# Folding one batch's first FFT stage onto 64x64 tiles, half of it inside a wait, with its input on two DMA queues

## The chip, the cores and the metric

One core of a Trainium2 chip (trn2) runs the whole program. The metric is device time in microseconds (us) of one execution; a time quoted for a kernel is the median of its fast runs, those within 1.5% of its fastest. In the profiles PE is TensorE (PEld its weight loads), DVE is VectorE, ACT ScalarE, POOL GpSimd and SP SyncE; SPq and ACTq are the queues (also rings) on which SP and ACT issue DMAs. Ratios are computed as the mean time of one kernel's fast runs over the mean of the other's fast runs of the same rounds, so they are not quite the ratio of the medians. The numbers in brackets behind a ratio are its 95% interval. Runs of different sessions are compared only through the kernel before, which ran beside each; its median was 904.68 us beside the kernel after, 901.19 beside e1 to e4, 901.86 beside e5 to e7 and 902.24 beside e8 to e11, and its single runs took 903.56 beside e12 and e13 and 908.88 beside e14 and e15.

## The reference, cut to what matters

```python
x: (8, 3008, 256)                      # batch, sequence, channels
X = np.fft.rfft(x, axis=1)             # filters: 1505 x 256
y = np.fft.irfft(X * (filt_r + 1j * filt_i), n=3008, axis=1)
h = y.reshape(24064, 256)
out = (np.maximum(h @ w_gate, 0) * (h @ w_val)) @ w_out    # d_ff 1536
```

The kernel splits 3008 = 94 x 32. Stage A is a 94-point transform (fp32 matmuls on the rows of `x`, one row per partition). Its result goes out to DRAM (`Abuf`) and comes back with the axes exchanged (`at`): this is the **bounce**. Then come a 32-point transform (`psX`), the product with the filters (`tt`, `uu`), the inverse of it (`psD`), a second trip through DRAM (`Dbuf` out, `dC` back), the last inverse step (`psY`), and the FFN (`psV`, `psG`, `psO`). The FFN loop of one batch has the FFT work of the next woven in. Only batch 0 has nothing to hide its FFT behind, and batch 1's A has to be done somewhere near it.

## The kernel before: the parts concerned

```python
def load_x(b, eng, cols):                 # 32 rows on every fourth of all partitions, 8 or 16 KB runs
    for c, c0, c1 in cols:
        for m in range(3):
            rows = min(32, B * N1 - (b * N1 + 32 * m))
            eng.dma_start(XF[c][m:m + 4 * rows - 3:4, c0:c1], ...)

def load_at(b, c):                        # bounce: 384 KB in 512 B pieces
    nc.sync.dma_start(ats[b][c:c + 125:4], _ap(Abuf[b], ..., [[D, 32], [4 * NC2 * D, NG], [1, D]]))
...
load_at(0, 0) ... load_at(0, 3)           # batch 0's four loads of A, on SP's queue
load_x(1, nc.sync, ((0, 0, 2 * q), (0, 2 * q, 4 * q), (1, 0, 4 * q)))     # then batch 1's x, same queue
early = items_a(1)                        # batch 1's A: 32 fp32 matmuls of 512 columns, unfolded
first_b(amid)                             # batch 0: psX, products, psD, with six matmuls of `early` amid
load_d(0, 0, 2)
nc.gpsimd.dma_start(last, ...)            # one row of D: Pool waits for D here
load_vg(DFF // 2, DFF)                    # second half of the gate and value weights
for f in early: f()                       # the remaining 26 matmuls, while D is away
item_c(0, 0); item_c(0, 1)                # psY, then the FFN loop
```

## Time and profile before

| | kernel before |
|---|---|
| median, runs | 903.77 us (900.53 to 905.6, 3 runs before the prediction); 904.68 with a fourth run of 907.75, used for the ratio |
| PE busy in the profiled run | 883.1 of 904.2 us |
| batch 0: end of A / first `psX` | 27.9 / 37.47 us |
| first `psV` (start of the FFN) | 63.38 us |
| first `psX` of batch 1 | 83.22 us |

The first 63 us are a chain of loads, bounce, products and the trip of D. The lines for this stand in the prediction. Two that it does not show: SP's timeline, which has start, length of the issue, operation and tile,

```profile
33.93 0.58 SPq L350 DMA_DIRECT2D at<-Abuf  x1
57.22 1.87 SPq L427 DMA_DIRECT2D dC<-Dbuf  x4
```

The fourth load of A is issued at 33.93, and PE's first `psX` follows at 37.47: it lands in some 3.5 us. SP issues the loads of D at 57.22, when D's last write has landed.

### The profile page before, as it was taken

How to read it: one execution, taken by the hardware profiler on the slowest of the kernel's cores; microseconds unless marked ns; L12 is line 12 of the kernel's file. 1: busy time of each engine (PE TensorE's matmuls, PEld its weight loads, DVE VectorE, ACT ScalarE, POOL GpSimd, SP SyncE). 2: the span in 40 equal slices, each digit the busy share in tenths (PEclk: the TensorE clock that was granted, in tenths of full speed). 3: DMA queues.
4: the chain of work that ended last, by engine and by line, in shares of the span. 5: the costliest groups of instructions: out<-in, count | busy, mean ns of one | idle time of the engine just before them, and what ended most of it. 6: DMA issues, size and time to landing. Idle time of an engine off the chain costs nothing.

```text
span 904.2 us, 19169 instructions
## 1 busy us (share of the span) xinstructions
PE 883.1 (98%) x7198; PEld 510.3 (56%) x7198; DVE 569.6 (63%) x873; ACT 498.8 (55%) x891; POOL 362.2 (40%) x359
## 2 busy tenths in 40 slices
PE   6899999999999999999999999999999999999997
PEld 2334555556555665566655566555655565666665
DVE  2636766467665776657766667666766577655553
ACT  3475555455655565555555565555565555555553
POOL 4242398217680386614864166811768000000001
PEclk9999999999999999999999999999999999999999
DMA  8998358523475344653364533754346512331111
GB/s 227 262 249 174 104 144 178 120 79 101 123 179 115 89 118 125 149 133 106 106 151 130 126 103 92 186 117 102 103 131 168 115 33 79 79 77 36 37 31 52
DMA packets 113554, 109.17 MB, mean 121 GB/s; under 512 B 20327, under 2 KB 98055, under 8 KB 112822
## 3 DMA queue, kind: packets, MB, share of 16 engines
q1 hardware_dynamic: 90294, 80.10, 34.4%
q0 software_dynamic: 22448, 26.41, 11.9%
q8 instruction: 56, 0.92, 0.4%
q10 hardware_dynamic: 720, 1.45, 0.4%
q14 instruction: 36, 0.29, 0.1%
HBM read 61.93 MB, written 49.81 MB: 124 GB/s over the span
## 4 chain that ended last, share of the span: by engine, by line
PE 85%; POOL 5%; DMA 5%; issue 3%; ACT 1%; SPq 1%; DVE 0%; ACTq 0%; POOLq 0%
PE psV L467 25%; PE psO L486 25%; PE psG L467 25%; PE psF L323 3%; PE psY L451 2%; PE psD L394 2%; PE psX L364 1%; DMA XP<-in_x_dram 1%; DMA WgT<-in_moe_w_gate_dram 1%; DMA Dbuf<-dsb 1%; PE psA L276 1%; POOL XP L296 1%; DMA XF<-in_x_dram 1%; POOL fold L309 1%; POOL XP L310 1%
## 5 line engine op out<-in xcount | busy, mean ns | idle before, releaser
L472 DVE SCALAR_TENSOR_TENSOR prod<-psG,vsb 128x512 bf16<-128x512 f32 x564 | 389.4, 690 | 267.5 <-ACT vsb L470 255.0
L470 ACT CAST vsb<-psV 128x512 bf16<-128x512 f32 x564 | 331.9, 588 | 269.4 <-PE psV L467 187.1
L467 PE MATMUL psV<-yT,WvT 128*128 128x512 bf16 x1128 | 337.1, 380 | 1.2 <-ACT yT L456 1.2
L467 PE MATMUL psG<-yT,WgT 128*128 128x512 bf16 x1128 | 336.1, 379 | 1.5 <-DMA WgT<-in_moe_w_gate_dram 0.7
L486 PE MATMUL psO<-WoT,prod 128*128 128x256 bf16 x2256 | 337.0, 273 | 0.0
L486 PEld LDWEIGHTS <-prod 128*128 128x128 bf16 x2256 | 220.8, 98 | 144.1 <-issue 0.8
L467 PEld LDWEIGHTS <-WgT 128*128 128x128 bf16 x1128 | 110.1, 98 | 137.1 <-issue 3.1
L467 PEld LDWEIGHTS <-WvT 128*128 128x128 bf16 x1128 | 98.5, 98 | 42.4 <-issue 30.9
L258 POOL CAST scr<-yT 128x8 f32<-128x8 bf16 x25 | 4.7, 189 | 268.1 <-ACT yT L456 268.1
L509 POOL DMA_DIRECT2D out_dram<-osb x5 | 2.6, 536 | 196.0 <-ACT osb L499 196.0
L380 DVE TENSOR_TENSOR tt<-psX,Ftr 128x512 bf16<-128x512 f32 x96 | 65.1, 683 | 6.7 <-PE psX L364 6.7
L499 ACT COPY osb<-psO 128x512 f32<-128x512 f32 x92 | 53.9, 585 | 27.7 <-PE psO L486 26.8
L309 POOL TENSOR_TENSOR fold<-XP 128x1024 f32<-128x1024 f32 x24 | 56.5, 2356 | 24.2 <-PE psF L323 20.8
L380 DVE TENSOR_TENSOR uu<-psX,Fti 128x512 bf16<-128x512 f32 x89 | 60.6, 681 | 0.0
L401 ACT CAST dsb<-psD 128x512 bf16<-128x512 f32 x96 | 51.5, 589 | 12.5 <-PE psD L394 11.8
L310 POOL TENSOR_TENSOR XP<-XP 128x1024 f32<-128x1024 f32 x24 | 56.4, 2348 | 1.9
L296 POOL DMA_DIRECT2D XP<-in_x_dram x96 | 56.7, 595 | 0.9 <-issue 0.4
L330 DVE CAST asb<-psF 128x512 bf16<-128x512 f32 x48 | 30.9, 686 | 21.3 <-PE psF L323 16.2
L330 ACT CAST asb<-psF 128x512 bf16<-128x512 f32 x48 | 25.8, 589 | 31.2 <-PE psF L323 31.2
L456 ACT CAST yT<-psY 128x512 bf16<-128x512 f32 x47 | 27.5, 585 | 25.3 <-PE psY L451 24.8
L458 DVE CAST yT<-psY 128x512 bf16<-128x512 f32 x47 | 32.0, 681 | 10.8 <-PE psY L451 10.8
L451 PE MATMUL psY<-M,dC 96*128 96x94 bf16 (+18 forms) x604 | 37.5, 198 | 0.1
(69 smaller groups left out, 505.5 us busy)
## 6 DMA issues: line engine op xcount, KB each, us to landing
at<-Abuf SPq DMA_DIRECT2D x32, 384.0 KB
dC<-Dbuf SPq DMA_DIRECT2D x64, 192.0 KB
XP<-in_x_dram POOLq DMA_DIRECT2D x48, 256.0 KB, 5.8
Dbuf<-dsb SPq DMA_DIRECT2D x23, 512.0 KB
XP<-in_x_dram POOLq DMA_DIRECT2D x96, 96.0 KB, 2.7
Abuf<-asb SPq DMA_DIRECT2D x96, 96.0 KB
out_dram<-osb SPq DMA_DIRECT2D x69, 94.0 KB
XF<-in_x_dram SPq DMA_DIRECT2D x15, 256.0 KB
```

Source lines behind the costliest of these rows:

```text
L296: nc.gpsimd.dma_start(xp[r:r + 24, 0:4:2, :], _ap(x, (b * N1 * N2 + o) * D, [[N2 * D, 24], [47 * N2 * D, 2], [1, 512]]))
L309: tt(t, xp[:, 0:2], xp[:, 2:4], op=ALU.add)
L310: tt(xp[:, 2:4], xp[:, 0:2], xp[:, 2:4], op=ALU.subtract)
L330: copy(asf[:, :, q, :], banks[q])
L380: nc.vector.tensor_tensor(p, psX, filt, op=ALU.mult)
L401: nc.scalar.copy(dsb[:, a, o:o + 2, :], psD[a])
L451: nc.tensor.matmul(psY[:, o:o + w], dCs[b, n2 // 8][:, n2 % 8, h * 128:(h + 1) * 128], M1[:, n1:n1 + w], start=True, stop=True)
L467: nc.tensor.matmul(pt[:, :W], w[:, h, ft * 128:(ft + 1) * 128], yt[:, h, :], start=(h == 0), stop=(h == 1))
L470: nc.scalar.copy(vsb, psV[:, :W])
L472: nc.vector.scalar_tensor_tensor(prod, in0=psG[:, :W], scalar=0.0, in1=vsb, op0=ALU.max, op1=ALU.mult)
L486: nc.tensor.matmul(psO[:, t % 2], prods[ft][:, t * 128:(t + 1) * 128], WoT[:, ft, :], start=(ft == 0), stop=(ft == NFT - 1))
L499: copy(osb[:, t0 % 2:t % 2 + 1], psO[:, t0 % 2:t % 2 + 1])
```

## The change

Batch 1's A is to use the symmetry of the real transform (fold rows n and −n into a sum and a difference, which halves the contraction) in four chunks on 64x64 tiles. Two chunks go into the wait for D, two into the FFN. VectorE folds chunks 0 and 1, GpSimd (POOL) folds 2 and 3. Its x is laid out for that: 48 rows for one half of the 32 columns on partitions 0 to 47, the same rows for the other half on partitions 64 to 111. It is split over SP's and ACT's queues, and starts right behind batch 0's third load of A; the fourth load of A moves to ACT's queue. In front, small zeroing and loads for the filters move behind batch 0's x. Filler, or junk, matmuls (`warm`, `psJ`) do no useful work; their results are thrown away.

```diff
+    def load_halves(c, engs):
+        for k in range(2):
+            for h in range(2):
+                engs[h].dma_start(X1[c][64 * h:64 * h + 48, k], _ap(x, ..., [[N2 * D, 48], [8 * D, 2], [1, 4 * D]]))
+    def fold_half(j, eng):
+        eng.tensor_tensor(t, xp[:, 0], xp[:, 1], op=ALU.add)
+        eng.tensor_tensor(xp[:, 1], xp[:, 0], xp[:, 1], op=ALU.subtract)
+    def halves_a(j):                      # sixteen matmuls, tile_position=(64 * h, 64 * e)
...
-    for (src, dst) in FILT:               # moved behind load_x(0, ...)
-        nc.vector.memset(dst[64:128, NG - 2:, :], 0.0)
-    load_own_filters()
...
-    load_x(1, nc.sync, ((0, 0, 2 * q), (0, 2 * q, 4 * q), (1, 0, 4 * q)))
+    load_at(0, 3, nc.scalar)
+    for c in range(2):
+        load_halves(c, (nc.sync, nc.scalar))
...
-    first_b(amid)
+    first_b()                             # filler matmuls in place of the six of A
     load_d(0, 0, 2)
+    for j in range(2):
+        fold_half(j, nc.vector)
+    for j in range(2, 4):
+        fold_half(j, nc.gpsimd)
     (the load named last, load_vg; load_o is now here too)
-    for i, f in enumerate(early): f() ...
+    warm(6)
+    for j in range(2):
+        halves_a(j)
+        warm(4)
...                                       # in the FFN of batch 0
+    for j, e in ((2, 1), (3, 3)):
+        at_step(e, lambda j=j: halves_a(j))
+    at_step(3, lambda: load_at_tiled(1))
```

More of the change, by code (lines that the diff above doesn't have):

```diff
@@ L105, in _tables @@
     fold = np.zeros((128, 4, 32))
+    half1 = np.zeros((128, 4, 32))
     i = np.arange(24)
@@ L115, in _tables @@
             fold[32 * q:32 * q + 24, 2 * odd + 1, 0:24] = np.where(k1 % 47 == 0, 0.0, -np.sin(th))
+        th = 2 * np.pi * (np.outer(np.arange(47) - 23, k1) % N1) / N1
+        for h in range(2):
+            half1[64 * h:64 * h + 47, 2 * odd, 0:24] = np.cos(th)
+            half1[64 * h:64 * h + 47, 2 * odd + 1, 0:24] = np.where(k1 % 47 == 0, 0.0, -np.sin(th))
     tab = np.concatenate([perm, swap, own.reshape(128, -1), m1], 1)
-    return wa.astype(np.float32), fold.reshape(128, 128).astype(np.float32), f2.astype(NBF16), tab.astype(NBF16)
+    fold = np.stack([fold, half1], 1).reshape(128, 256)
+    return wa.astype(np.float32), fold.astype(np.float32), f2.astype(NBF16), tab.astype(NBF16)
 @with_exitstack
@@ L155 @@
     Dbuf = [dram.tile([NROW * N2, D], BF16, name=f"Dbuf{b}") for b in range(B)]
-    XF = [pro.tile([128, NX2 * D], FP32, name=f"XF{c}") for c in range(N2 // NX2)]
+    XF = [consts.tile([128, NX2 * D], FP32, name=f"XF{c}") for c in range(N2 // NX2)]
+    XD = [t[:, :].rearrange("p (k n) -> p k n", k=4) for t in XF]
+    XP = [XD[j // 2][:, :, 512 * (j % 2):512 * (j % 2) + 512] for j in range(4)]
     WA = pro.tile([128, NROW], FP32)
-    WF = consts.tile([128, 4, 32], FP32)
+    WFS = consts.tile([128, 2, 4, 32], FP32)
+    WF, W1 = WFS[:, 0], WFS[:, 1].rearrange("p c k -> p (c k)")
     M1 = consts.tile([NROW, N1], BF16)
@@ L182 @@
     FILT = ((filt_r, Ftr), (filt_i, Fti))
+    junk = pro.tile([128, 512], BF16, tag="junk", bufs=1)
     tabs = pro.tile([128, tab_h.shape[1]], BF16, tag="tabs", bufs=1)
@@ L261, with fft_tag @@
     turn = {"tags": ("fft", "psv", "psg", "pso"), "i": 0}
-    def fft_tag(side=False):
-        if side and turn.get("side"):
-            return turn["side"]
+    def fft_tag():
         turn["i"] += 1
@@ L273, in one @@
                 st["asb"] = sb.tile([128, NC2 * D], BF16, tag="asb", bufs=4, name="asb")
-            psA = ps.tile([128, 512], FP32, tag=fft_tag(True), name="psA")
+            psA = ps.tile([128, 512], FP32, tag=fft_tag(), name="psA")
             o = (c * NC2 % NX2) * D + j * 512
@@ L280, in one @@
             if j == 3:
-                eng = nc.scalar if b and c > 1 else nc.sync
-                eng.dma_start(_ap(Abuf[b], c * NROW * NC2 * D, [[NC2 * D, NROW], [1, NC2 * D]]),
+                nc.sync.dma_start(_ap(Abuf[b], c * NROW * NC2 * D, [[NC2 * D, NROW], [1, NC2 * D]]),
                                   st["asb"][:NROW])
@@ L306, in fold_chunk @@
         xp = XP[j]
-        t = fs.tile([128, 2, 512], FP32, tag="fold", bufs=2, name="fold")
+        t = sb.tile([128, 2, 512], FP32, tag="fold", bufs=2, name="fold")
         tt = nc.gpsimd.tensor_tensor
@@ L325, in tiled_a, with store_a @@
                                  tile_position=(r, 32 * c))
+        store_a(b, j, banks, (nc.scalar.copy, nc.vector.tensor_copy) * 2)
+    def store_a(b, j, banks, copies):
         asf = sb.tile([128, NC2 * D], BF16, tag="asb", bufs=4, name="asb")
@@ L328, in tiled_a @@
         for q in range(4):
-            copy = nc.scalar.copy if q % 2 == 0 else nc.vector.tensor_copy
-            copy(asf[:, :, q, :], banks[q])
+            copies[q](asf[:, :, q, :], banks[q])
         for c in range(4):
@@ L342, in load_at_tiled, with load_at @@
                                   [[D, 32], [N2 * D, 24], [1, D]]))
-    POOL_U = ((0, 1), (1, 0), (1, 1), (2, 0), (2, 1), (3, 1), (4, 0))
+    X1 = [t[:, :].rearrange("p (k q n) -> p k q n", k=2, q=2) for t in XF]
+    def load_halves(c, engs):
+        for k in range(2):
+            for h in range(2):
+                engs[h].dma_start(X1[c][64 * h:64 * h + 48, k],
+                                  _ap(x, ((N1 + 47 * k) * N2 + 16 * h + 4 * c) * D,
+                                      [[N2 * D, 48], [8 * D, 2], [1, 4 * D]]))
+    def fold_half(j, eng):
+        xp = X1[j // 2][:, :, :, 2 * D * (j % 2):2 * D * (j % 2) + 2 * D]
+        pool, tag = (pro, "half") if j < 2 else (sb, "fold")
+        t = pool.tile([128, 2, 2 * D], FP32, tag=tag, bufs=2, name="half")
+        eng.tensor_tensor(t, xp[:, 0], xp[:, 1], op=ALU.add)
+        eng.tensor_tensor(xp[:, 1], xp[:, 0], xp[:, 1], op=ALU.subtract)
+        fold[1, j] = (t, xp[:, 1])
+    def halves_a(j):
+        banks = [ps.tile([128, 2, D], FP32, tag=t, name="psF") for t in ("psv", "psg", "fft", "fft")]
+        for q in range(2):
+            for h in range(2):
+                for e in range(2):
+                    nc.tensor.matmul(banks[2 * h + q][64 * e:64 * e + 64],
+                                     W1[64 * h:64 * h + 48, 64 * e:64 * e + 64],
+                                     fold[1, j][e][64 * h:64 * h + 48, q], start=True, stop=True,
+                                     tile_position=(64 * h, 64 * e))
+        store_a(1, j, banks, (nc.scalar.copy,) * 4 if j < 2 else (nc.scalar.copy, nc.vector.tensor_copy) * 2)
+    POOL_U = ((0, 1), (1, 0), (1, 1), (2, 1), (3, 0), (3, 1))
     ats = {}
-    def load_at(b, c):
+    def load_at(b, c, eng):
         if c == 0:
             ats[b] = sb.tile([128, NG, D], BF16, tag="at", bufs=1, name="at")
-        nc.sync.dma_start(ats[b][c:c + 125:4],
+        eng.dma_start(ats[b][c:c + 125:4],
                           _ap(Abuf[b], c * NROW * NC2 * D, [[D, 32], [4 * NC2 * D, NG], [1, D]]))
@@ L354, with fwd @@
     CUTS = (0, 2, 4, 6)
-    def fwd(b, i):
+    def fwd(b, i, junks=False):
         for e in range(2):
-            psXs[b, i, e] = ps.tile([128, 2, D], FP32, tag=fft_tag(), name="psX")
+            tag = "fft" if b or not e else "psv"
+            psXs[b, i, e] = ps.tile([128, 2, D], FP32, tag=tag, name="psX")
+            for _ in range(2 * junks):
+                nc.tensor.matmul(psXs[b, i, e], junk[:, 0:128], junk, start=True, stop=True)
         for m in range(2):
@@ L381, in product, with inv @@
         tus[b, i, e, k] = p
-    def inv(b, i, tags=None, cuts=CUTS):
+    def inv(b, i, tags, cuts=CUTS):
         if i in cuts:
@@ L387, in inv @@
         i0, dsb = dsbs[b]
-        psD = [ps.tile([128, 2, D], FP32, tag=tags[a] if tags else fft_tag(), name="psD")
+        psD = [ps.tile([128, 2, D], FP32, tag=tags[a], name="psD")
                for a in range(2)]
@@ L404, in inv, with first_b @@
                               dsb[:, :, :o + 2, :])
-    def first_b(amid):
-        cuts = (0, 2, 4, 5, 6)
+    def first_b():
+        cuts, tags = (0, 2, 4, 5, 6), ("psg", "pso")
         for i in range(6):
-            fwd(0, i)
+            fwd(0, i, True)
             if i > 1:
-                inv(0, i - 2, cuts=cuts)
+                inv(0, i - 2, tags, cuts)
             for e in range(2):
@@ L415, in first_b @@
                 product(0, i, e, 1, pool=(i, e) in POOL_U)
-            amid(i)
-        inv(0, 4, cuts=cuts)
-        amid(6)
-        inv(0, 5, cuts=cuts)
+        for i in range(4, 6):
+            inv(0, i, tags, cuts)
     dCs = {}
@@ L511, in o_part @@
                                           osb[o + c0:o + c1, tt % 2])
-    junk = pro.tile([128, 512], BF16, tag="junk", bufs=1)
     def warm(n, cols=512):
-        psJ = ps.tile([128, 512], FP32, tag=fft_tag(True), name="psJ")
+        psJ = ps.tile([128, 512], FP32, tag=fft_tag(), name="psJ")
         for i in range(n):
@@ L538 @@
     load_x(0, nc.sync, ((0, 0, q), (0, q, 2 * q), (0, 2 * q, 4 * q), (1, 0, 2 * q), (1, 2 * q, 4 * q)))
-    nc.sync.dma_start(WF, nc.inline_tensor(fold_h, name="dft_fold").ap())
+    nc.sync.dma_start(WFS, nc.inline_tensor(fold_h, name="dft_fold").ap())
+    for (src, dst) in FILT:
+        nc.vector.memset(dst[64:128, NG - 2:, :], 0.0)
+    load_own_filters()
     hold_gpsimd(XF[0][:, 2 * q - 8:2 * q])
@@ L547 @@
         if i == 12:
-            load_at(0, 0)
-            load_at(0, 1)
-    for c in range(2, 4):
-        load_at(0, c)
+            load_at(0, 0, nc.sync)
+            load_at(0, 1, nc.sync)
+    load_at(0, 2, nc.sync)
     for half in range(2):
@@ L564 @@
     place_nyq()
-    for i in range(11):
+    for i in range(13):
         warm(2)
-    load_x(1, nc.sync, ((0, 0, 2 * q), (0, 2 * q, 4 * q), (1, 0, 4 * q)))
-    early = items_a(1)
-    def amid(i):
-        if i < 2:
-            warm(4, 256)
-        else:
-            for _ in range((1, 1, 2, 1, 1)[i - 2]):
-                next(early)()
+    load_at(0, 3, nc.scalar)
+    for c in range(2):
+        load_halves(c, (nc.sync, nc.scalar))
     hold_gpsimd(ats[0][0:32, NG - 1, 0:8])
     load_vg(0, DFF // 2)
-    turn["tags"], turn["side"] = ("fft", "psv", "psg"), "pso"
-    first_b(amid)
-    turn["tags"], turn["side"] = ("fft", "psv", "psg", "pso"), None
+    first_b()
     load_d(0, 0, 2)
+    for j in range(2):
+        fold_half(j, nc.vector)
+    for j in range(2, 4):
+        fold_half(j, nc.gpsimd)
     nc.gpsimd.dma_start(pro.tile([1, D], BF16, tag="last", bufs=1, name="last"),
@@ L586 @@
     load_vg(DFF // 2, DFF)
-    load_at(1, 0)
-    for i, f in enumerate(early):
-        f()
-        if i == 5:
-            load_at(1, 1)
+    load_o()
+    warm(6)
+    for j in range(2):
+        halves_a(j)
+        warm(4)
     for h in range(2):
         item_c(0, h)
-    hold_gpsimd(yTs[0][:, 0, 0:8])
-    load_o()
     prologue.close()
     fs = ctx.enter_context(tc.tile_pool(name="fs", bufs=2))
-    XP = []
-    def clear_chunks():
-        for i in range(4):
-            XP.append(fs.tile([128, 4, 512], FP32, tag=f"XP{i}", bufs=1, name=f"XP{i}"))
-            nc.gpsimd.memset(XP[i], 0.0)
     turn["tags"] = ("fft",)
@@ L613 @@
     C_AT = (8, 10)
-    at_step(2, clear_chunks)
     for b in range(1, B):
@@ L617 @@
         if b == 1:
-            for c in range(2, 4):
-                at_step(c - 2, lambda c=c: load_at(1, c))
+            for j, e in ((2, 1), (3, 3)):
+                at_step(e, lambda j=j: halves_a(j))
+            at_step(3, lambda: load_at_tiled(1))
         else:
```

## The prediction

> **What bounds the kernel now.** I read the page first. Its busy row and its chain say that TensorE is the bound of the whole run: PE is busy 98% of 904.2 us, and 85% of the chain that ended last is PE work.
>
> ```profile
> PE 883.1 (98%) x7198; PEld 510.3 (56%) x7198; DVE 569.6 (63%) x873; ACT 498.8 (55%) x891; POOL 362.2 (40%) x359
> PE 85%; POOL 5%; DMA 5%; issue 3%; ACT 1%; SPq 1%; DVE 0%; ACTq 0%; POOLq 0%
> ```
>
> So a change can move the end in two ways only: by moving the instant at which the FFN loop starts, or by adding to or taking from PE's time inside the loop. The change touches only the first 100 us or so. I read PE's timeline there, then the waits of PE from 36 to 92 us:
>
> ```profile
> 19.11 8.78 PE L276 MATMUL psA<-XF,WA 128*96 128x512 f32 x16 [2.06 <-DMA XF<-in_x_dram]
> 37.47 0.41 PE L364 MATMUL psX<-at,F 64*64 64x256 bf16 x8 [2.01 <-issue]
> 52.91 8.82 PE L276 MATMUL psA<-XF,WA 128*96 128x512 f32 x20
> 63.38 0.59 PE L467 MATMUL psV<-yT,WvT 128*128 128x512 bf16 x2 [1.18 <-ACT yT L456]
> 83.22 0.41 PE L364 MATMUL psX<-at,F 64*64 64x256 bf16 x8 [0.86 <-issue]
> ...
> PE psG L467 <- DMA WgT<-in_moe_w_gate_dram: 0.7, 1, 0.7
> ```
>
> The FFN starts at 63.38. Before it PE runs batch 1's A (the second psA row): 8.8 us of fp32 matmuls that stand exactly where D of batch 0 goes to memory and back. The chain of waits shows that round trip:
>
> ```profile
> 46.00 7.34 DMA Dbuf<-dsb
> ...
> 54.53 2.67 DMA Dbuf<-dsb
> ...
> 59.06 10.74 DMA WgT<-in_moe_w_gate_dram
> ```
>
> The last write of D lands at 57.2, SP issues the loads of it by 59.1, so D is back near 60 us by my estimate; A ends at 61.7. The two finish almost together: PE's A is hardly longer than the wait it fills. Removing A alone therefore buys at most some 2 us.
>
> [...] eight 64x256 bf16 matmuls (psX) take 0.41 us. [...] No two-SBUF-input op of DVE is in the trace before; its PSUM product of 512 elements takes 0.69, so I estimate 1.15 us for 1024. [...] from 44 to 45 us q1 and q0 moved 28 packets each, but 0.29 and 0.04 MB, so large packets take the bandwidth.
>
> **The change, part by part.**
>
> Front. The zeroing for the filters and their small loads move behind the x loads, so DVE clears the first quarter of XF 0.8 us sooner and POOL, which idled until 1.43 and cleared the second quarter at 4.07 to 5.07, does so about 2.5 us sooner. SP's fourth load waited for that until 5.10; now it can follow the third at about 3.6. From 10 us on the DMA is full (0.99 to 1.19), which limits the gain: some 1.4 us on batch 0's A.
>
> Bounce of batch 0. Batch 1's x no longer queues behind the whole bounce. SP's half follows the third load of A, into a hole: the DMA share from 33 to 35 us is 0.06. But the fourth load of A, issued at 33.93 on SP, goes to ACT's ring, in 512 B packets against x's 4 KB on SP's. By packet-wise turns it gets an eighth while x lasts: I estimate 0.5 to 1.8 us more. With 1.4 gained in front, the first psX starts at 37.3, near the 37.47 of before. The filler added ahead (four plus four junk matmuls) ends by then.
>
> Forward and inverse FFT of batch 0. Six psA (6 x 0.86 = 5.2 us of PE) and their ACT copies (6 x 0.57 = 3.4 us) go, 24 junk matmuls (24 x 0.216 = 5.2 us) come, so PE is even and ACT, busy 13.7 of 18 us, is freed. Pool products fall from 7 to 6. Walking the six rounds by 0.61 us per DVE product, 0.55 per ACT copy and 1.15 per Pool product, the last product ends 13.2 us after the first psX (before: 14.4) and the last inverse 13.9 after. The 7.34 us wait for the first write of D shrinks as x is no longer ahead of it in SP's ring. The last copy of D ends at 51.9 instead of 54.5, its write lands at 54.6, D is back near 57.5.
>
> The wait for D. DVE folds chunks 0 and 1 after its products: 4 x 1.15 = 4.6, from 50.5 to 55.1. POOL folds 2 and 3: 4 x 2.35 = 9.4, from 47 to 56.6. A chunk's matmuls are eight 64x512 fp32 on four tiles, two rounds of 0.86 plus some 0.2 (before, sixteen on 32x32 tiles, one round, took 1.16): 1.9 us. PE: inverse to 51.3, six junk (1.3), chunk 0 to 54.6, four junk (0.9), chunk 1 55.1 to 57, four junk to 57.9, then psY and a copy: FFN at 59.6. The one-row load named last now waits for POOL's folds: issued at 57.2, landing 3.4 later (as before), at 60.6, and the first copy out of psV waits for it. Effective start 60.2: 3.2 us gained.
>
> Inside the FFN. Chunks 2 and 3 add 2 x 1.9 = 3.8 us of PE. Two waits should go: 0.86 for A of batch 1 (written by about 73, wanted near 82) and perhaps the 0.7 for the second half of the gate weights, whose load is issued at the same time as before; the four memsets of POOL (7.1 us) vanish, off the path. The chunk stores are sixteen small DMAs on an SP queue with time to spare.
>
> Sum: -3.2 + 3.8 - 0.9 - 0.5 = -0.8; from there on the loop is the same, instruction for instruction but for line numbers, with the folds of batch 2 on strided views of the same sizes. Total about 903.
>
> **Rivals.** (A) [...] POOL's folds begin at 47 and DVE's at 50.5; if each excludes the other for a whole op, they alternate and DVE's four end near 61 instead of 55. Chunk 1 then ends at 63, the FFN starts at 65, and the total is 907 to 910, more if PE's idle stretch drops the clock. [...] Against: the amounts of filler fit folds of 1.15 us too well, as if chosen from a trace that did not have it. I give it 45%. (B) The granted clock. From 19 to 24 us it was 0.66 after a DMA wait, and again from 166 to 171; at half rate for some 3.5 us each cost about 1.8 us. Other arrival times of x could spare the first or add one: plus or minus 1.8 us. (C) The bounce is slowed more than I think, and all that follows slips: plus 1 to 2. (D) The gate weights come later, because POOL must fold before it can issue them: plus 1 to 3 on the sixth step.
>
> **Range and chances.** Without (A) 901 to 903.5, with it 906 to 910; the clock adds 1.8 either way, and three runs of before spread over 5 us. Median 903; eight in ten between 898 and 909. Two per cent is 18 us; nothing above reaches that, since all that changes lies within the first 85 us, where PE already idles only about 9 us.
>
> **What would show each step.** First psX at 37.3, within 1 (front and bounce); last product 13.2 after it; DVE folds of 1.15 each and back to back (no lock) or with gaps of 2.4 (lock); first psV between 59 and 61 (no lock), 64 to 66 (lock); psF rows of about 1.9 us a chunk; no idle before the psX of batch 1 near 82. I am wrong if DVE's folds stretch in themselves, if psX starts after 39, if the weights stall step 6 for over 1 us, or if the loop after 100 us runs at another pace.

## The result, and the profile after

The kernel after took 918.14 us (917.25 to 918.98, 4 runs) and the kernel before, in the same rounds, 904.68 (900.53 to 907.75, 4 runs). The ratio is 1.0152, with a 95% interval of 1.0108 to 1.0195. Results are correct. The whole interval lies above 1: the change costs 1 to 2%, and the time is 15 us more than predicted.

| us from the start (profiled runs) | before | after | later by |
|---|---|---|---|
| end of batch 0's A | 27.9 | 25.2 | −2.7 |
| first `psX` | 37.47 | 46.51 | +9.0 |
| first `psV` | 63.38 | 77.78 | +14.4 |
| first `psX` of batch 1 | 83.22 | 100.12 | +16.9 |
| end | 904.2 | 915.8 | +11.6 |

PE's timeline of the kernel after, the lines that answer to those in the prediction (start, busy time, line, operation, and in brackets the idle time before it with what ended it):

```profile
18.16 7.08 PE L284 MATMUL psA<-XF,WA 128*96 128x512 f32 x16 [2.47 <-DMA XF<-in_x_dram]
46.51 0.64 PE L408 MATMUL psX<-at,F 64*64 64x256 bf16 x8 [11.15 <-DMA at<-Abuf]
77.78 0.38 PE L509 MATMUL psV<-yT,WvT 128*128 128x512 bf16 x1 [0.25 <-ACT yT L498]
100.12 0.41 PE L408 MATMUL psX<-at,F 64*64 64x256 bf16 x8
```

PE now stands still for 11.15 us ahead of the first `psX`, for a load of A. The chain of waits of the kernel after names which one (start, length, what):

```profile
25.88 6.47 DMA Abuf<-asb
32.35 0.02 issue
32.38 14.09 DMA at<-Abuf
46.47 0.04 issue
46.51 0.70 PE psX L408 x7
```

The load issued at 32.38 is the fourth, on ACT's queue. It takes 14.09 us; before, its twin took some 3.5. What the DMA engines did meanwhile shows in two rows of the windows view of each kernel (window, its length, busy time of PE, PEld, DVE, ACT and POOL, then PEclk, the clock granted to TensorE as a share of full speed, then the mean busy share of the 16 DMA engines, and what all queues together moved in GB/s). First the kernel before:

```profile
36.00:39.00 3.00, 1.53 (x23) 0.91 (x24) 1.09 (x2) 0.00 (x0) 1.20 (x3) 1.00 0.99 324
45.00:48.00 3.00, 2.92 (x28) 1.14 (x29) 2.15 (x4) 2.86 (x6) 2.29 (x3) 1.00 1.02 353
```

Then the kernel after:

```profile
36.00:39.00 3.00, 0.00 (x0) 0.00 (x0) 0.00 (x0) 0.00 (x0) 0.00 (x0) 1.00 1.03 135
45.00:48.00 3.00, 1.49 (x11) 0.56 (x12) 0.81 (x2) 0.00 (x0) 1.11 (x3) 0.50 1.02 212
```

The engines are as full as before (1.03 against 0.99) and move 135 GB/s instead of 324. The DMA view of the kernel after says whose bytes they are (queue, packets, MB, share), first from 34 to 37 us:

```profile
q1 hardware_dynamic: 128, 0.44, 101.7%
q10 hardware_dynamic: 4, 0.00, 0.6%
```

Then from 37 to 40 us:

```profile
q10 hardware_dynamic: 442, 0.23, 64.2%
q1 hardware_dynamic: 67, 0.20, 44.5%
```

q1 is SP's queue with x, q10 is ACT's with the load of A (and ACT's half of x behind it). In the first three us q10 moves 4 packets against 128; in one-us views all four of them fall between 36 and 37, after SP had issued the last of its four loads of x (28.71 to 35.93). In the next three us q10 moves 442 against 67. So the load of A first stood still and then got most of the packets. By an estimate from packets and MB, all but some twenty of its 768 packets had moved by 42 us, but the load is complete only at 46.47. The last row of the windows view above shows the second cost, PEclk at 0.50: TensorE, idle since 35 us, was granted half rate from 42 us on (0.68 from 39 to 42), and was still at 0.62 from 48 to 51.

Later the folds show a third cost. VectorE's timeline:

```profile
59.95 1.22 DVE L369 TENSOR_TENSOR half<-XF 128x1024 f32<-128x1024 f32 x1
61.20 3.25 DVE L370 TENSOR_TENSOR XF<-XF 128x1024 f32<-128x1024 f32 x1
64.37 3.38 DVE L369 TENSOR_TENSOR half<-XF 128x1024 f32<-128x1024 f32 x1
67.78 3.25 DVE L370 TENSOR_TENSOR XF<-XF 128x1024 f32<-128x1024 f32 x1
```

GpSimd's timeline:

```profile
57.67 2.35 POOL L369 TENSOR_TENSOR half<-XF 128x1024 f32<-128x1024 f32 x1
60.10 3.27 POOL L370 TENSOR_TENSOR XF<-XF 128x1024 f32<-128x1024 f32 x1
63.33 3.34 POOL L369 TENSOR_TENSOR half<-XF 128x1024 f32<-128x1024 f32 x1
66.75 3.20 POOL L370 TENSOR_TENSOR XF<-XF 128x1024 f32<-128x1024 f32 x1
```

Only VectorE's first fold, which starts in the tail of POOL's first, has the length that it has alone, 1.22 us. Each later one lasts until the POOL fold beside it ends and then some 1.1 us more: VectorE's four end at 71.03 instead of some 64.8 (59.95 plus four times 1.2). That is rival (A) of the prediction, called the lock from here on: side by side VectorE's folds take 3.25 to 3.38 us (1.22 alone) and POOL's 3.20 to 3.34 (2.35 alone). It shows as longer instructions and not as gaps of 2.4 us between them, which the prediction had told its reader to look for.

### The profile page after: what moved, and what is told of

Same layout as the page of the kernel before. It is cut to its first block, busy times and chain, and to the rows that moved or that the text cites.

```text
span 915.8 us, 19321 instructions
## 1 busy us (share of the span) xinstructions
PE 888.0 (97%) x7264; PEld 510.3 (56%) x7264; DVE 583.3 (64%) x882; ACT 496.2 (54%) x886; POOL 365.7 (40%) x357
## 4 chain that ended last, share of the span: by engine, by line
PE 87%; DMA 4%; POOL 4%; DVE 2%; SPq 1%; issue 1%; ACT 0%; DVEq 0%; POOLq 0%
PE psV L509 26%; PE psG L509 25%; PE psO L528 25%; PE psF L330 3%; PE psY L493 2%; DMA XF<-in_x_dram 2%; PE psD L438 2%; PE psX L408 2%; DMA at<-Abuf 2%; PE psF L379 1%; PE psA L284 1%; SPq L185 1%; DVE XF L370 1%; DMA Abuf<-asb 1%; POOL XF L303 1%
## 5 line engine op out<-in xcount | busy, mean ns | idle before, releaser
L316 POOL TENSOR_TENSOR fold<-XF 128x1024 f32<-128x1024 f32 x24 | 56.5, 2355 | 21.0 <-PE psF L330 20.8
L303 POOL DMA_DIRECT2D XF<-in_x_dram x96 | 56.6, 595 | 1.6 <-PE psG L509 1.2
L317 POOL TENSOR_TENSOR XF<-XF 128x1024 f32<-128x1024 f32 x24 | 56.4, 2348 | 1.9
L340 ACT CAST asb<-psF 128x512 bf16<-128x512 f32 x60 | 32.2, 589 | 40.8 <-PE psF L330 28.7
L340 DVE CAST asb<-psF 128x512 bf16<-128x512 f32 x52 | 33.5, 686 | 20.8 <-PE psF L330 11.6
L498 ACT CAST yT<-psY 128x512 bf16<-128x512 f32 x47 | 27.5, 585 | 25.2 <-PE psY L493 25.0
L493 PEld LDWEIGHTS <-dC 96*128 96x128 bf16 x604 | 34.9, 98 | 3.5 <-issue 1.1
```

What stands on the lines that cost most here:

```text
L303: nc.gpsimd.dma_start(xp[r:r + 24, 0:4:2, :], _ap(x, (b * N1 * N2 + o) * D, [[N2 * D, 24], [47 * N2 * D, 2], [1, 512]]))
L316: tt(t, xp[:, 0:2], xp[:, 2:4], op=ALU.add)
L317: tt(xp[:, 2:4], xp[:, 0:2], xp[:, 2:4], op=ALU.subtract)
L340: copies[q](asf[:, :, q, :], banks[q])
L493: nc.tensor.matmul(psY[:, o:o + w], dCs[b, n2 // 8][:, n2 % 8, h * 128:(h + 1) * 128], M1[:, n1:n1 + w], start=True, stop=True)
```

## The experiments

Theory at the outset (**T1**): the fourth load of A starves behind x on the shared DMA engines; x itself is slow. Rivals: the lock of the folds is the main loss (**T2**), the cold clock is (**T3**), or the way the change moves the front (**T4**). All kernels but the four spoilt ones (e6, e7, e12, e13) are in this table. The DMA rate is the mean of four 3 us windows from 39 to 51 us, in which the share was mostly near full; it is of all queues together, so x is only part of it. "One" marks a single run, whose state is unknown and whose ratio is not given.

| run | first psX | DMA rate, GB/s | first psV | time | ratio to before |
|---|---|---|---|---|---|
| before | 37.47 | 304 | 63.38 | 904.68; 901.19 to 908.88 beside other runs | 1 |
| after | 46.51 | (see above) | 77.78 | 918.14 | 1.0152 |
| e1 A's load first, one queue | 36.27 | 192 | 67.51 | 910.78 | 1.0103 |
| e2 all folds on VectorE | 47.21 | – | 70.35 | 915.59 | 1.0159 |
| e3 before, x in bands of 32 | 37.29 | 219 | 67.15 | 908.6 | one |
| e4 before, new front only | 35.82 | – | 62.94 | 901.16 | 1.0004 |
| e5 A first, x on two queues, folds on VectorE | 37.57 | 170 | 67.62 | 912.34 | 1.0114 |
| e8 before, 4 KB runs | 37.26 | 267 | 64.35 | 902.91 | one |
| e9 bands of 32, 4 KB runs | 36.98 | 238 | 66.52 | 905.54 | one |
| e10 A first, x spread, folds on VectorE | 37.62 | 223 | 64.35 | 909.3 | 1.0097 |
| e11 as e10, four chunks ahead | 36.21 | – | 66.06 | 908.73 | 1.0068 |
| e14 before, x in bands of 48 | 37.37 | 168 | 74.28 | 913.82 | one |
| e15 before, 48 rows on every second partition | 36.25 | 237 | 65.10 | 904.61 | one |

e3, e9 and e12 to e15 give a wrong result on purpose: x lands on other partitions than the tables of A expect.

**e1: the load of A first.**

```diff
-    load_at(0, 3, nc.scalar)
+    load_at(0, 3, nc.sync)
-        load_halves(c, (nc.sync, nc.scalar))
+        load_halves(c, (nc.sync, nc.sync))
```

> The changed kernel with the fourth load of A issued on SP right behind the third, and all eight x loads behind it on SP's queue. Theory (ring sharing: A's last load starves in 512 B packets beside x's 4 KB packets): the first psX starts at 35.5 to 37.5 us instead of 46.5. x then starts 5 us later and comes at 0.15 to 0.25 MB/us from one queue, so it lands near 50 to 57 and the folds wait for it; FFN start 66 to 73 instead of 77.8, time 907 to 913. Rival (A's last load was late because x into 48 neighbouring partitions clogs the engines, whatever the ring): first psX stays after 42.

PE's timeline:

```profile
36.27 0.41 PE L408 MATMUL psX<-at,F 64*64 64x256 bf16 x8 [1.33 <-DMA at<-Abuf]
```

The first `psX` came at 36.27, as forecast, and the ratio fell to 1.0103 (1.0086 to 1.012; the kernel after's 1.0108 to 1.0195 overlaps it a little). So running beside x is what delayed the load of A. Whether x being slow or the second queue did it, e1 does not say: it takes x away altogether while A loads. The DMA engines still moved only 169 to 217 GB/s from 39 to 54 us, and D's writes, behind x on SP's queue, became the next wait. PE's waits from 30 to 100 us (us in total, times, longest):

```profile
PE psJ L560 <- ACT dsb L445: 4.6, 1, 4.6
PE psX L408 <- DMA at<-Abuf: 2.8, 2, 1.5
PE psF L379 <- ACT vsb L512: 1.2, 1, 1.2
```

POOL's folds started late, at 57.02, so VectorE's were alone this time: 1.22 us each. e1 thus took away the lock as well. Of the 10.3 us that it gained at the FFN's start, 5.2 are left at the end of the profiled runs.

**e2: all folds on VectorE.**

```diff
     for j in range(2, 4):
-        fold_half(j, nc.gpsimd)
+        fold_half(j, nc.vector)
```

> The changed kernel with all four chunks folded on DVE, none on POOL. [...] each of DVE's eight operations takes 1.15 to 1.25 us instead of 3.3, chunk 1 is ready 6 us sooner, FFN starts near 70 instead of 77.8, and the time falls by 6 to 8 us to some 910 to 912. Rival (DVE's operations are slow for another reason, such as x still landing or the strided view): they stay over 2 us and the time is the same or worse, as DVE has twice the folds.

VectorE's timeline:

```profile
61.90 1.22 DVE L370 TENSOR_TENSOR XF<-XF 128x1024 f32<-128x1024 f32 x1
63.05 1.22 DVE L369 TENSOR_TENSOR half<-XF 128x1024 f32<-128x1024 f32 x1
```

Without POOL beside it a fold takes 1.22 instead of 3.25 to 3.38: the lock is shown, and the FFN starts 7.4 us sooner than in the kernel after. Yet the ratio is 1.0159 (1.0144 to 1.0174): no better. In the profiles the gain shrinks at each milestone: 5.4 us in batch 1's first round of `psX`, after a wait, 3.7 us at its last round, 2.6 us at the first of batch 2. It is given back to a wait of 1.6 us for batch 1's A, and to the clock, which averaged 0.83 over the ten us round it and made the round of `psX` after it 8.88 instead of 7.21 us. T2 alone is refuted: the lock costs the folds what it was said to cost, but little of that reaches the end. The intervals of the two ratios would hide a gain of the 2.6 us that the profiles show.

**e3: only the placement of x, in the kernel before.**

```diff
-                eng.dma_start(XF[c][m:m + 4 * rows - 3:4, c0:c1],
+                eng.dma_start(XF[c][32 * m:32 * m + rows, c0:c1] if b else XF[c][m:m + 4 * rows - 3:4, c0:c1],
```

> The kernel before with one thing changed: batch 1's x goes into 32 neighbouring partitions per load instead of every fourth (wrong result on purpose; same bytes, packets and queue). Theory (partitions): the rate of these loads falls from about 0.33 MB/us to 0.15 to 0.2, the psA among the FFT wait for x and the time rises by 3 to 8 us. Rival (the slow rate of x in the changed kernel came from its 4 KB packets or its queues): rate and time as before.

The DMA rate fell to 200 to 245 GB/s (39 to 51 us) and the FFN's start slipped from 63.38 to 67.15. Placement counts. It does not fall to the 146 that SP's band of the changed layout moved from 34 to 37 us.

**e4: only the new front, in the kernel before.** The diff is the moved zeroing and filter loads shown above.

> The kernel before with only the front of the change: the filters' zeroing and small loads behind the x loads. Expected: batch 0's psA end near 25.2 as in the changed kernel (27.9 before), first psX 1.0 to 2.0 us sooner (35.5 to 36.5), and 1 to 2 us less time (902 to 903 where before is 904); a rival, that D's round trip and not this sets the FFN start, would leave the time as before.

The first `psX` came 1.65 us sooner (35.82), the FFN 0.44 us sooner (62.94), and the ratio is 1.0004 (0.9989 to 1.0018). The front gain is real and no gain is seen at the end: PE waited 2.95 us ahead of `psX`, and the clock fell below full rate (0.5 to 0.7 from 36 to 45 us). The trip of D, the rival in the forecast, did not set the rest: SP issued the loads of D at 56.15 (57.22 before), and PE ran batch 1's A from 52.47 (52.91 before) without a gap up to `psY`:

```profile
52.47 8.82 PE L276 MATMUL psA<-XF,WA 128*96 128x512 f32 x20
```

T4 is out.

**e5: ACT's queue held until A is in.**

```diff
-    load_at(0, 3, nc.scalar)
+    load_at(0, 3, nc.sync)
+    held = sb.tile([128, 8], FP32, tag="held", bufs=1, name="held")
+    nc.scalar.copy(held[:32], ats[0][0:32, NG - 1, 0:8])
     (folds of chunks 2 and 3 on nc.vector)
```

> The changed kernel with A's fourth load on SP before x, ACT's half of x held until that load has landed, and all folds on DVE. First psX near 36.3 as when all x stood behind the bounce; the two halves of x then run side by side from two queues at some 0.25 MB/us (one alone: 0.15) and land near 49, when DVE gets to the folds; folds of 1.22 us; FFN start 59 to 62, time 1 below to 3 above the kernel before. If x still crawls at 0.15 to 0.18, FFN start stays near 67 and the partitions alone are not the reason.

Both halves of x ran side by side on two queues at 153 to 191 GB/s, no faster than in e1. So neither the number of queues nor running the lower and the upper band at once helps. VectorE waited 3.22 us for x. By the forecast's last sentence this outcome speaks against the partitions as the only reason; e14 and e15 show what they do on their own.

**e6 and e7: two misses.** Both tried to spread x (e6 on every fourth partition, e7 on all 128), with one transfer for both halves, so that the outermost dimension of the source had size 2:

```diff
+                    engs[k].dma_start(X1[c][m:m + 125:4, k, q],
+                                      _ap(x, ..., [[16 * D, 2], [N2 * D, 16], [1, 4 * D]]))
```

> Both causes taken away: A's fourth load and then all of x on SP's queue, x spread over every fourth partition so that a load reaches both halves of the partitions, all folds on DVE. First psX 36.3; x at 0.3 MB/us, landed by 47 to 49; folds of 1.22 us from 49.5; FFN start 58.5 to 60.5; 2.5 us more between FFN start and batch 1's first psX than before; time within 2 us of the kernel before (so 0.998 to 1.002 of it). If it stays 5 us or more above, a third cause is still hidden.

> The changed kernel with only the placement of x altered: each of the eight loads takes 128 partitions (64 rows of both halves, 4.2 MB in all instead of 3.1, 4 KB packets still), queues, order and folds as in the changed kernel. It parts the two shares of the late A: ring sharing stays, slow x goes. Expected first psX at 38 to 40.5 (46.5 in the changed kernel, 36.3 with A ahead): if so, 2 to 4 us of the delay are ring sharing at full rate and 6 to 8 the slow partitions; if it stays above 44, placement has nothing to do with it. DVE's folds stay at 3.3 us beside POOL's.

The windows view of e6 (columns as above):

```profile
60.00:80.00 20.00, 4.63 (x16) 1.39 (x17) 4.81 (x4) 0.00 (x0) 0.00 (x0) 0.58 0.13 53
```

From 60 to 80 us the DMA share was 0.13 at 53 GB/s in e6, and 0.13 at 51 GB/s in e7; e6's x took until about 100 us, and the kernels 957.8 and 979.61 us. e10, with the same rows of x in transfers whose outermost size is 16 and whose runs are 16 KB instead of 4, had a share of 0.87 to 1.14 and 199 to 251 GB/s (39 to 51 us). Why e6 and e7 ran at such a share is not shown. Both runs say nothing about placement, and e7 leaves open what it was built for: how much of the late load of A is the slow x and how much the second queue.

**e8 and e9: are the short runs to blame?** In the changed layout x is read in runs of 4 KB, 8 KB apart; before, in 8 and 16 KB. e8 is the kernel before with such runs, e9 is e3 with them.

```diff
+                    xv = XF[c][m:m + 4 * rows - 3:4].rearrange("p (a s n) -> p a s n", a=2, s=2)
+                    eng.dma_start(xv[:, :, s], _ap(x, ..., [[N2 * D, rows], [8 * D, 2], [1, 4 * D]]))
```

> The kernel before, with batch 1's x in 12 transfers of 0.25 MB whose runs in memory are 4 KB, 8 KB apart, as in the kernel after; it still lands on every fourth partition, and the result stays correct. The open question: why the kernel after's x ran at about 0.145 MB/us (141 to 149 GB/s at a full DMA share) where the kernel before's ran at 249 to 353 GB/s. If the small runs in memory cause it alone, the DMA engines are full at under 200 GB/s while x loads here too and the start of the FFN comes 4 to 8 us later than the kernel before's 63.4. If the neighbouring partitions cause it alone, the rate is that of the kernel before (250 to 350 GB/s) and the FFN starts at 63 to 64.5. Mine: mostly the partitions, so 230 to 330 GB/s here.

> The same small runs, and batch 1's x on neighbouring partitions in three bands of 32 (wrong result on purpose). With the 16 and 8 KB runs the neighbouring partitions alone gave 200 to 257 GB/s. If the two slow each other down, this shows 140 to 190 GB/s at a full share, the kernel after's rate, and an FFN start at 68 or later. If the small runs do nothing, it shows 200 to 257 GB/s again and an FFN start at about 67, and what made the kernel after still slower than that is the form of its own transfers (48 partitions) or the write traffic beside it.

e8 kept 267 GB/s and an FFN start at 64.35 (its slow first stretch, 191 GB/s from 39 to 42, had a share of 0.76 only). e9, at 238, was no slower than e3's 219. The short runs are not the cause.

**e12 to e15: bands of 48.** What remained was 48 rows on neighbouring partitions. e12 put x of the kernel before into bands of 48 and 46 rows, e13 the same rows on every second partition.

> The kernel before with batch 1's x in two bands of 48 and 46 neighbouring partitions from 0 and from 64, as the kernel after places it, but in the long runs of before (8 and 16 KB), all on one queue and with the folding of before (wrong result on purpose). [...] Then the DMA engines show a full share at 150 to 195 GB/s from 36 on, x takes some 18 us, the first chunk of A and the writes of D slip, and the FFN starts at 68 to 73. If instead it is the form of after's transfers (two pieces a row) or its mixing of two queues that made it slower than 200 to 257 GB/s, this run shows that rate again and an FFN start near 67.

> As the run before it, with the same transfers of 48 and 46 rows, on every second partition instead (0, 2 to 94, then 1, 3 to 91), wrong result on purpose. [...] the share-filled stretch shows 260 to 350 GB/s, as before, and the FFN starts at 63 to 65. If 48-row transfers are slow whatever the partitions, it shows under 200 GB/s and the FFN starts at 68 or later.

Both were spoilt: with transfers of 46 rows in them they again ran at a share of 0.13 (51 to 57 us: 44 and 45 GB/s in e12, 43 and 45 in e13), and the kernels took 934.0 and 929.81 us. e14 and e15 repeat them with 48 rows throughout, and in those six us their share is 0.72 to 1.09:

```diff
-                rows = 48 - 2 * m
+                rows = 48
```

> The run with bands of 48 and 46 again, with 48 rows in both transfers: [...] 150 to 200 GB/s at a full share from 39 to 54, and an FFN start at 67 to 72. If bands of 48 are no slower than bands of 32, 200 to 257 GB/s and an FFN start near 67 or before.

> As the run before it (two transfers of 48 rows), on every second partition: 0, 2 to 94 and 1, 3 to 95. [...] 250 to 350 GB/s at a full share, FFN start at 63 to 65.5, x all in by about 48. If transfers of 48 rows are slow whatever the partitions: under 200 GB/s and an FFN start at 67 or later.

The windows view of e14:

```profile
39.00:42.00 3.00, 2.33 (x33) 1.12 (x36) 3.00 (x6) 1.76 (x3) 1.69 (x3) 0.72 1.08 175
42.00:45.00 3.00, 2.41 (x37) 0.93 (x29) 1.40 (x3) 2.53 (x5) 3.00 (x3) 1.00 1.10 180
45.00:48.00 3.00, 2.92 (x30) 1.26 (x29) 2.32 (x5) 2.83 (x6) 2.42 (x3) 1.00 1.02 156
48.00:51.00 3.00, 3.00 (x33) 1.10 (x35) 1.85 (x4) 2.80 (x7) 1.15 (x1) 1.00 1.21 161
```

The windows view of e15:

```profile
39.00:42.00 3.00, 2.65 (x31) 1.08 (x34) 2.06 (x4) 2.36 (x6) 2.72 (x3) 0.84 1.22 309
42.00:45.00 3.00, 2.37 (x37) 1.08 (x37) 1.89 (x3) 2.85 (x7) 2.91 (x3) 1.00 0.93 209
45.00:48.00 3.00, 2.92 (x36) 1.20 (x33) 1.89 (x3) 2.85 (x7) 1.66 (x2) 1.00 0.99 209
48.00:51.00 3.00, 3.00 (x44) 1.16 (x32) 2.49 (x4) 2.81 (x6) 0.65 (x1) 1.00 1.05 220
```

The same transfers of 48 rows ran at 156 to 180 GB/s in bands and at 209 to 309 on every second partition. The placement in bands of 48 is the cause: on its own it moves the FFN's start by 9.2 us (74.28 in e14 against 65.10 in e15; 10.9 against the kernel before, which has other transfers too). The forecast for e15 hit the FFN's start and missed the rate of 250 to 350; the one for e14 hit the rate up to 51 us (133 and 127 followed) and missed the start. The times of these single runs decide nothing: the kernel before took 908.88 beside them, between e15's 904.61 and e14's 913.82.

The mean rates from 39 to 51 us, with other traffic in them, rank the placements: 168 GB/s in bands of 48 (e14), 219 in bands of 32 (e3), 237 on every second partition (e15), 304 on every fourth over all 128 (the kernel before). For x alone there are two figures: 175 and 180 where e14 moved it with both bands in one queue (39 to 45 us), and 146 for SP's band in the kernel after (34 to 37 us). Both bands at once on two queues (e5: 170) did not double that. Why a placement has the rate that it has is not shown by any run.

**e10 and e11: a mended version of the change.** A's load first and all of x on SP's queue in 16 KB runs, each transfer 16 rows on every fourth partition of its half; all folds on VectorE. The forecast took the load of A beside a slow x and the lock of the folds for the whole loss. e11 also computes all four chunks ahead of the FFN.

```diff
+                eng.dma_start(XF[k][64 * h + m:64 * h + m + 61:4],
+                              _ap(x, ..., [[N2 * D, 16], [1, 16 * D]]))
...
-    for j in range(2):                    # e11
+    for j in range(4):
         halves_a(j)
```

> The kernel after with four things changed: batch 0's last load of A ahead of x on the same queue, all x on that queue, x's rows on every fourth partition of each half in 12 transfers of 16 partitions with 16 KB runs (the table of the fold permuted to match), and all folds on VectorE. [...] Then x loads at over 280 GB/s and is in by 48, the first product-side matmul of the inverse stage comes at 36 to 37, folds last 1.22 us each from about 50, the FFN starts at 58.5 to 61.5, and the two chunks inside the FFN (3.8 us) and a wait for batch 1's A (1.5) give back most of it: 897 to 904 against 901 to 905 of the kernel before, ratio 0.994 to 1.002. Rival: the fold path itself, filler and cold clock hold the FFN start above 63.4, and the ratio is over 1.004.

> As the run before this, with all four chunks of batch 1's A computed ahead of the FFN and its load of A at an early FFN step. The folds end near 54.5 and D comes in after that, so I expect the FFN start at 59.5 to 62.5 and nothing paid within the FFN: from the FFN's start to batch 1's first inverse-stage matmul 18.2 to 19.8 us, and 895 to 901 us, ratio 0.991 to 0.999 against the kernel before. If the wait for D has no room for two more chunks, the FFN start moves by the full 3.8 us against the run before this and the ratio is the same as its.

Ratios 1.0097 (1.0061 to 1.0132) and 1.0068 (1.0054 to 1.0082): still worse than the kernel before; e11 is better than the change, and e10's interval overlaps with the change's 1.0108 to 1.0195. I had expected the FFN at 58.5 to 62.5. It started at 64.35 in e10, where PE waited 2.1 us for D, and at 66.06 in e11. There PE did not wait for D: the four chunks filled it up to `psY`, and their folds began at 52.04, after VectorE had waited 2.6 us for x (e10: 52.60, after 1.8). POOL's timeline of e10 shows when D's last write had landed, since its one-row load waits for that:

```profile
59.84 0.57 POOL L618 DMA_DIRECT2D last<-Dbuf  x1 [11.32 <-DMA Dbuf<-dsb]
```

In the kernel before the same line stands at 57.77. A spread within 64 partitions still loads at 223 GB/s, and D's writes queue behind x: ACT waited 4.6 us (e10) and 5.5 us (e11) for a D buffer to be written out. In e11 PE then also waited for batch 1's A:

```profile
PE psX L409 <- DMA at<-Abuf: 4.0, 1, 4.0
```

The folded chunks leave by sixteen small stores on SP's queue (from 60.8 to 74.3 us in e11) ahead of that load.

## Why the prediction was wrong, by its own steps

**Front: right in sign, too small, and no gain at the end.** 1.4 us were predicted for batch 0's A, 2.7 came. e4 has it alone, at a ratio of 1.0004 (0.9989 to 1.0018).

**Bounce: the step that failed.** It put "0.5 to 1.8 us more" on the fourth load of A and the first `psX` at 37.3. The load took 14.09 us, and `psX` came at 46.51, 9.2 us late. It is past the prediction's own sign of being wrong (after 39). Two things were mis-sized. The step has no rate for x in the new layout; the only one that the prediction reads is of the old (0.29 MB from 44 to 45 us), while the profile after shows 0.145 MB/us. And the step's own rule, an eighth of the bandwidth while x lasts, was not carried through. At 324 GB/s an eighth is about 40, and the load has 0.39 MB, which is some 10 us if x lasts that long; SP's half of x, 1.5 MB, lasts 5 us even at the old rate. So 1.8 was never an upper end. The rule itself failed too. It was the estimate from one us of the profile before, in which two queues moved 28 packets each (44 to 45 us), and the load of A did not get an eighth: it got nothing until 36 us, then most of the packets (442 against 67 from 37 to 40), and was complete only at 46.47. Rival (C), "plus 1 to 2", is what came true, at about nine.

**FFT of batch 0: right.** Last product 13.5 us after the first `psX` (13.2 predicted).

**D back at 57.5: right counted from the first `psX`, but not reached when mended.** In the kernel after SP issued the loads of D at 64.60, 18.1 us after the first `psX`, where 17.3 was predicted (54.6 less 37.3); the folds, not D, held PE there. The step rested on a DMA that is done with x. In e10 and e11 the last write landed at 59 to 60 us, 22 to 23 us after the first `psX`, not 17.3.

**Folds and lock: rival (A), given 45%, came true.** Alone 1.22 us (1.15 estimated) and 2.35 for POOL, as written; side by side 3.25 to 3.38. VectorE's four took 11.1 us, 6.2 more than alone. The cold clock (PEclk 0.50 and 0.58 there) added about 3, where rival (B) allowed 1.8: chunk 1's matmuls took 3.78 us instead of 1.88, its filler 1.89 instead of about 1.0. From the first `psX` to the FFN it made 31.3 us in place of 22.9 (37.3 to 60.2): 8.4 late. Together with the bounce that is 17.6 us. One sum of the prediction slips here, without effect: it has chunk 1 start at 55.1, though the four filler matmuls ahead of it end at 55.5 by its own figures.

**Inside the FFN: right in sum.** A chunk took 1.88 us, and from the FFN's start to batch 1's `psX` PE needed 22.34 instead of 19.84: +2.5, with +2.4 predicted (3.8 − 0.9 − 0.5). But the waits vanished only because everything else was ready by then: with an earlier FFN, a wait for batch 1's A came back (1.0 us in e10, 1.6 in e2, 4.0 in e11).

**The sum.** −0.8 predicted, plus 17.6, makes +16.8 at batch 1's first `psX`, where +16.9 was measured. Of this 11.6 us are left at the end of the profiled runs and 13.5 between the medians. Part of the difference is chance in the profiled run before: from batch 1's last `psX` to batch 2's first it took 69.9 us, where e4, with the same loop, took 66.5 and the kernel after 65.4; the granted clock was 0.66 from 166 to 171 us there. Set against e4's profile instead, the kernel after is 18.1 us later at batch 1's first `psX` and 16.2 at the end. The remaining 2 us are not settled.

**What stays open.** How much of the late load of A is due to x being slow and how much to its standing on a second queue: no run that came out right has one without the other. How much of the end the lock and the clock cost separately: e2 removes the lock and the end hardly follows, and no run holds the clock up. Why ACT's queue moved nothing before 36 us, and its last packets only at 46.47. Why x is slower in bands (168 GB/s in e14, 219 in e3) than on every fourth partition (304). And why e6, e7, e12 and e13 ran at a share of 0.13.

## What to carry to other kernels

Before re-laying a load for the sake of the arithmetic, measure the load on its new partitions alone, and see what else is in flight: here the layout that halved a contraction has bands of 48, which in e14 loaded at 168 GB/s where the kernel before had 304, and what shared the DMA engines paid (the load of A took 14.09 us instead of some 3.5). A short, urgent load is safer ahead of a bulk load on the same queue than beside it on a second one: here its first user started at 36.27 instead of 46.51. Work that is taken off PE where PE only fills a wait buys little until the wait itself (here D's trip through DRAM, behind x) gets shorter: in e10 PE then waited 2.1 us for D.
